# Decode attention with a gated MLP on one core: the first V's load without gate, V31 in halves, wo in seven pieces, loads issued by GpSimd

## The chip, the core and the metric

The kernel runs on one core of a Trainium2 chip. A core has TensorE (PE, matrix products into eight PSUM banks), VectorE (DVE), ScalarE (ACT), GpSimd (POOL) and SyncE (SP), each with an instruction stream of its own; they meet at semaphores. Sixteen DMA engines carry data between device memory (HBM) and the on-chip SBUF of 128 partitions. SyncE, ScalarE and GpSimd can issue loads. The metric is device time of one execution in microseconds.

## The reference

One decode step for two batch rows: attention over a cache of 8192 keys with 32 heads of 128, multiplied by the gate of a small MLP, with a residual. All in float32.

```python
xn = layernorm(x)                                  # x (2, 1, 512)
q = (xn @ wq) as (2, 32 heads, 1, 128)
p = softmax(q . k_cache * 128 ** -0.5)             # k_cache (2, 32, 8192, 128)
s = (p @ v_cache) as (2, 1, 4096) @ wo             # wo (4096, 512)
y = layernorm(xn)
g = silu(gelu_tanh(y @ w1 + b1) @ w2 + b2)         # w1 (512, 1376), w2 (1376, 512)
return x + s * g
```

K and V are 268 MB each; every byte is used once.

## The kernel before, in words

K and V are cut into N = 32 loads each of 8.39 MB: two heads of one batch row a load, 64 partitions for each head, 128 keys in a partition, so a partition receives one contiguous row of 64 KB. In the text K0 to K31 and V0 to V31 are these loads.

Three buffers of that size take turns (lines 120 to 140). KBUF[0] and KBUF[1] take K's even and odd loads; KBUF[1] holds wq first, so K1 is loaded only after the q product (event pq). The third, VB, takes every V but the last, one after the other. Before V0, VB is the home of many small tiles of the start (`boot`): w1, w2, x, xn, y, b2, the copy of q, the selection matrix `sel`, q_all, and `z` and `th` of the gate. V31 goes into KBUF[0], free after K30, and wo into VB after V30.

`op` (line 41) issues one instruction with its waits; `take` (line 38) waits for a count and subtracts it, for use inside the TensorE loop. Line 51 in the profile is the line in `op` that increments the semaphore, so nearly all instructions carry it; they are told apart by tile names.

The order of the work:

- **Start.** SyncE issues w1, w2, the biases, wq and K0 in this order (lines 182 to 189). Layernorms, the w1 product, gelu and the q product follow as these land. Then 64 rows of q are spread to all partitions (`queries`, tiles Q, through banks PB in turn), and w2's product, event `pgate`, ends TensorE's setup. ScalarE copies it to `z` and takes tanh of half of it to `th` (lines 262, 263).
- **Each load n (lines 270 to 306).** VectorE multiplies K by q in place and adds up each key's 128 products (two operations over 16384 elements a partition), then takes the maximum over keys (MX), which TensorE transposes and spreads back (`softmax`), and ScalarE makes the exponentials PZ. TensorE multiplies them with V (`weighted`: 32 products into bank `po`, event p_v; the profile has two rows for each float32 product), ScalarE copies `po` to o4, and TensorE picks each head's own products out of it (event p_t).
- **Loads.** K of n + 2 is issued when the reduction of n is done (k_done); V of n + 1 when the products with V of n are done (p_v). Both are on SyncE, in that order, so a waiting one holds up those behind it.
- **gate and V0 (lines 283 to 290).** In the turn of n = 0, after MX and its negated copy, VectorE computes `gate` = (th + 1) * z. SyncE waits for gate, the last copies of q and pgate, and then issues V0, since z and th lie in VB.
- **End.** V31 is one load; wo comes in four pieces, at columns WO_CUTS of the 32 blocks of rows that lie in a partition, issued after V30's products. After the last product with V, heads are gathered and scaled to `on`, which is multiplied by wo into `acc` (128 small products, 256 rows of the profile; each piece is waited for by itself); VectorE multiplies by gate and adds x, and the result is stored.

PSUM bank 0 is both one of the two PB banks and later `po`, so it is zeroed by VectorE (t["po0"], line 258) after the last q copies from it and ahead of K0's multiplication in VectorE's stream. Bank 4 is `acc` and, early, the place of q's selection (pqa), zeroed after that (t["acc0"], line 259).

Of the kernel before, what the change touches and what calls it, by code (L numbers as in the profile page):

```python
# [13 lines left out]
class Program:  # L14
# [24 lines left out]
    def wait(self, eng, *tokens):  # L39
        for name, v in self.need(eng, tokens):  # L40
            self.engines[eng].wait_ge(self.sem(name), v)

    def take(self, eng, name, v=1):

        self.engines[eng].wait_ge(self.sem(name), v).then_inc(self.sem(name), -v)  # L45

    def op(self, eng, method, *args, waits=(), sig=None, quiet=False, **kwargs):
        need = self.need(eng, waits)
        for name, v in need[:-1]:
            self.engines[eng].wait_ge(self.sem(name), v)  # L50
        ins = getattr(self.engines[eng], method)(*args, **kwargs)  # L51
        for name, v in need[-1:]:
            ins._wait_ge(self.sem(name), v)
        if quiet:
            return None
        name = sig or "own_" + eng
        by = 16 if method == "dma_start" else 1
        ins.then_inc(self.sem(name), by)
        self.counts[name] += by
        return name, self.counts[name]  # L60


def decode_kernel(nc, x, kc, vc, wq, wo, w1, b1, w2, b2, out):
    P = 128
# [4 lines left out]
    U = 2  # L69
    HP = P // U  # L70
    KP = S // HP
    HH = H // U
    N = B * HH
# [5 lines left out]
    JW = 512 // DH  # L79
# [4 lines left out]
    OC = DH // PH  # L84
    BH = B * H
    NPB = 512 // DH
    WO_CUTS = (0, 24, 29, 31, 32)

    pr = Program(nc)
    op, wait, take = pr.op, pr.wait, pr.take  # L90

    def sb(shape, name):
        return nc.alloc_sbuf_tensor(name, list(shape), F32).ap()
# [4 lines left out]
    kf = kc.rearrange("b h s d -> (b h s d)").rearrange("(n p j d) -> n p j d", p=P, j=KP, d=DH)  # L98
    vf = vc.rearrange("b h s d -> (b h s d)").rearrange("(n p j d) -> n p j d", p=P, j=KP, d=DH)
# [3 lines left out]
    KBUF, VB = rows[:2], rows[2]  # L103
    used = [0]

    def boot(p, n):
        a = used[0]
        used[0] += n
        assert used[0] <= KP * DH
        return big[2][:p, a:a + n]  # L110
# [6 lines left out]
    b2_sb = boot(1, D)  # L117
    q_nat = boot(P, NG // QT * 512).rearrange("p (n c) -> p n c", c=512)
    sel = boot(P, P)
    z = boot(P, P)  # L120
    th = boot(P, P)
    q_all = boot(BH, DH)
    wq_sb = big[1].rearrange("p (c n) -> p c n", n=H * DH)
    wo_sb = big[2].rearrange("p (c n) -> p c n", n=D)

    Q = sb([P, N, DH], "Q")
# [4 lines left out]
    mod = sb([P, R], "mod")  # L131
# [3 lines left out]
    x4 = sb([P, P], "x4")  # L135
    gate = sb([P, P], "gate")
    res = sb([P, P], "res")
    xnT = sb([P, ND, B], "xnT")
    yT = sb([P, ND, B], "yT")
    hT = sb([P, NF + 1, B], "hT")  # L140
# [13 lines left out]
    on = sb([P, B, OC], "on")  # L154

    bank = [ps([P, 512], f"bank{i}") for i in range(8)]
    po = bank[0]
# [3 lines left out]
    acc = bank[4][:, :P]  # L161
    OA = bank[5][:, :B * (OC + 1)].rearrange("p (b c) -> p b c", c=OC + 1)
    pgate = bank[6][:, :P]
    ph = bank[7][:, :(NF + 1) * B]
    PQ = [bank[1], bank[2]]
    pxn, py = bank[3][:, :ND * B], bank[5][:, :ND * B]
    pqa = bank[4][:, :P]
    PB = [bank[0], bank[7]]

    PE_EVENTS = ["xnT", "yT", "ph", "pq", "pqa"] + [f"pb{g}" for g in range(N // NPB)] + ["pgate"]  # L170

    def pe(name):
        return "pe_setup", PE_EVENTS.index(name) + 1

    def pe_n(name, n):
        return name, n + 1

    t = {}
# [7 lines left out]
    op("SP", "dma_start", b1_sb[:, NF:], b1[F - P:, None], sig="d_b")  # L186
    t["b"] = op("SP", "dma_start", b2_sb, b2[None, :], sig="d_b")
    op("SP", "dma_start", wq_sb, wq.rearrange("(p c) n -> p c n", p=P), sig="d_wq")
    k_land = {0: op("SP", "dma_start", KBUF[0], kf[0], sig="d_k0")}
    t["x4m"] = op("DVE", "memset", x4, 0.0)  # L190
    for b in range(B):
        t["x4"] = op("ACT", "dma_start", x4[b::R, :], x[b, 0].rearrange("(j n) -> j n", n=P), sig="d_x4",
                     waits=[t["x4m"]])


    a = op("POOL", "memset", ident, 0.0)
# [7 lines left out]
    a = op("DVE", "memset", half, 0.0)  # L204
    for s in range(U):
        t["half"] = op("DVE", "memset", half[HP * s:HP * (s + 1), PH * s:PH * (s + 1)], 1.0, waits=[a])
    a = op("DVE", "memset", sel, 0.0)
    for k in (1, 2, 6):
        t["mem"] = op("DVE", "memset", bank[k], 0.0)
    by_row = ident.rearrange("p (j r) -> p r j", r=R)  # L210
    t["mod"] = op("DVE", "tensor_reduce", out=mod, in_=by_row, axis=AX.X, op=ALU.add, waits=[t["ident"]])
# [1 line left out]
                  op=ALU.add)  # L213
    t["sel"] = op("DVE", "tensor_copy",
                  sel[:, HP:].rearrange("p (b j r) -> p b j r", b=B, r=HG)[:, :, :QT, 0], by_row[:, :B, :],
                  waits=[a])
# [4 lines left out]
    def layernorm(dst, src, name, after):  # L221
# [16 lines left out]
    a = op("DVE", "tensor_tensor", out=gh, in0=ph.rearrange("p (f b) -> p f b", b=B),  # L238
           in1=b1_sb.unsqueeze(2).to_broadcast([P, NF + 1, B]), op=ALU.add, waits=[pe("ph"), t["b"]])
    c = op("DVE", "tensor_mul", gu, gh, gh, waits=[a])  # L240
    c = op("DVE", "tensor_scalar", gu, gu, GELU_A, 1.0, op0=ALU.mult, op1=ALU.add, waits=[c])
    c = op("DVE", "tensor_mul", gu, gu, gh, waits=[c])
# [10 lines left out]
    for g in range(N // NPB):  # L253
        t[f"Q{g}"] = op("ACT", "copy", Q[:, g * NPB:(g + 1) * NPB, :],
                        PB[g % 2].rearrange("p (n d) -> p n d", d=DH), waits=[pe(f"pb{g}")])
        for n in range(g * NPB, (g + 1) * NPB):
            Qt[n] = t[f"Q{g}"]
    t["po0"] = op("DVE", "memset", po, 0.0, waits=[t[f"Q{N // NPB - 2}"]])
    t["acc0"] = op("DVE", "memset", acc, 0.0, waits=[t["qall"]])


    t["z"] = op("ACT", "copy", z, pgate, waits=[pe("pgate")])
    t["th"] = op("ACT", "activation", th, z, AF.Tanh, scale=0.5, waits=[t["z"]])


    op_k1 = op("SP", "dma_start", KBUF[1], kf[1], sig="d_k1", waits=[pe("pq"), ("d_wq", 16)])
    k_land[1] = op_k1

    pending = {}
    for n in range(N):  # L270
        k = KBUF[n % U]
        if n:

            op("ACT", "copy", o4, po, sig="s_o4", waits=[pe_n("p_v", n - 1)])
            t["OT"] = op("ACT", "copy", OT[:, U * (n - 1):U * n], pt[:, :U], waits=[pe_n("p_t", n - 1)])
        qb = Q[:, n, :].unsqueeze(1).to_broadcast([P, KP, DH])
        a = op("DVE", "tensor_tensor", out=k, in0=k, in1=qb, op=ALU.mult, waits=[k_land[n], Qt[n]])
        a = op("DVE", "tensor_reduce", out=SC[n % 2], in_=k, axis=AX.X, op=ALU.add, waits=[a], sig="v_k")
        k_done = a
        op("DVE", "tensor_reduce", out=MX, in_=SC[n % 2], axis=AX.X, op=ALU.max, waits=[a], sig="v_mx")  # L280
        op("DVE", "tensor_reduce", out=nm, in_=pm[:1, :P].rearrange("o (s r) -> o s r", s=U), axis=AX.X,
           op=ALU.max, negate=True, waits=[pe_n("p_m", n)], sig="v_nm")
        if n == 0:
            a = op("DVE", "scalar_tensor_tensor", gate, th, 1.0, z, op0=ALU.add, op1=ALU.mult,
                   waits=[t["th"], t["pool"]])
            t["gate"] = a

            wait("SP", t["gate"], t["sel"], t["qnat"], pe("pgate"))
            op("SP", "dma_start", VB, vf[0], sig="d_v")
            t["v_last"] = None  # L290
        a = op("ACT", "copy", bias, pn[:, :1], waits=[pe_n("p_n", n)])
        sc = SC[n % 2].rearrange("p (t j) -> p t j", j=JW)
        for s in range(U):
            r = slice(HP * s, HP * (s + 1))
            op("ACT", "activation", PZ[r, :, s, :], sc[r], AF.Exp, bias=bias[r], scale=SCALE,
               accum_out=RS[r, n:n + 1], waits=[a, t["pool"]], sig="s_pz")
        m = n + 2
        if m < N:
            k_land[m] = op("SP", "dma_start", KBUF[m % U], kf[m], sig=f"d_k{m % U}", waits=[k_done])
            op("SP", "dma_start", VB, vf[m - 1], sig="d_v", waits=[pe_n("p_v", m - 2)])  # L300
        elif m == N:
            op("SP", "dma_start", KBUF[m % U], vf[N - 1], sig="d_v31", waits=[k_done])
            wait("SP", pe_n("p_v", N - 2))
            wo_v = wo.rearrange("(p c) n -> p c n", p=P)
            for i, (c0, c1) in enumerate(zip(WO_CUTS, WO_CUTS[1:])):
                op("SP", "dma_start", wo_sb[:, c0:c1], wo_v[:, c0:c1], sig=f"d_wo{i}")
    op("ACT", "copy", o4, po, sig="s_o4", waits=[pe_n("p_v", N - 1)])
    t["OT"] = op("ACT", "copy", OT[:, U * (N - 1):], pt[:, :U], waits=[pe_n("p_t", N - 1)])

# [7 lines left out]
    t["on"] = op("DVE", "tensor_tensor", out=on, in0=OA[:, :, :OC], in1=rl.unsqueeze(2).to_broadcast([P, B, OC]),  # L317
                 op=ALU.mult, waits=[a])
    a = op("DVE", "scalar_tensor_tensor", res, acc, 0.5, gate, op0=ALU.mult, op1=ALU.mult,
           waits=[pe_n("p_acc", 0), t["gate"], t["acc0"]])  # L320
    t["res"] = op("DVE", "tensor_add", res, res, x4, waits=[a, t["x4"]])
    for b, eng in enumerate(("SP", "ACT")):
        t[f"o{b}"] = op(eng, "dma_start", out[b, 0].rearrange("(j n) -> j n", n=P), res[b::R, :], sig=f"d_o{b}",
# [70 lines left out]

    def weighted(v, last=False):
        take("PE", "s_pz", U)
        if last:
            nc.tensor.wait_ge(pr.sem("d_v31"), 16)
        else:
            take("PE", "d_v", 16)  # L400
        for i in range(NT):
            j = i % QT
            mm(po[R * j:R * j + U * JW, :], PZ[:, i].rearrange("p s j -> p (s j)"),
               v[:, i * JW:(i + 1) * JW, :].rearrange("p j d -> p (j d)"), start=i < QT, stop=i + QT >= NT,
               sig="p_v" if i == NT - 1 else None)
        take("PE", "s_o4")
        for i in range(JW):
            mm(pt[:, :U], o4[:, i * DH:(i + 1) * DH], mod[:, i:U * JW:JW], start=i == 0, stop=i == JW - 1,
               sig="p_t" if i == JW - 1 else None)

    wait("PE", t["po0"], t["pool"], t["mod"])
    softmax()
    with nc.tensor.Fori(0, N - 1):
        weighted(VB)
# [8 lines left out]
    for i, (c0, c1) in enumerate(zip(WO_CUTS, WO_CUTS[1:])):  # L423
        for c in range(c0, c1):
            for j in range(QT):
                last = c == OC - 1 and j == QT - 1
                mm(acc[R * j:R * j + B, :], on[:, :, c], wo_sb[:, c, j * P:(j + 1) * P], start=c == 0,
                   stop=c == OC - 1, waits=[t["on"], t["acc0"], (f"d_wo{i}", 16)], sig="p_acc" if last else None)


_INS = ["A_x", "A_k_cache", "A_v_cache", "A_wq", "A_wo", "B_w1", "B_b1", "B_w2", "B_b2"]
# [23 lines left out]
```

## Time and profile before

| | us |
|---|---|
| median of three runs | 1325.63 |
| lowest and highest | 1323.99 and 1325.75 |
| the profiled execution | 1324.34 |
| its span, first to last instruction | 1322.9 |
| VectorE busy in it | 1129.2 |
| TensorE busy in it | 396.9 |
| ScalarE busy in it | 70.5 |
| GpSimd busy in it | 1.1 |

Loads move 559.37 MB, 423 GB/s over the span. Times in the profile count from the first instruction. A row of the timeline gives start, duration, engine, line, operation, the tile written and those read, how many such instructions were merged, and in brackets how long the engine had been idle and what ended it. SPq marks SyncE's issuing of a load. A row of DMA issues ends with the time from issue to landing. A row of stretches gives length, busy time (and count) of PE, PEld, DVE, ACT and POOL, the granted TensorE clock, the busy share of the DMA engines and GB/s; a packet's bytes are counted where it begins.

### The profile page before, as it was taken

The page shows a single profiled execution, that of the slowest core. Times are in us where ns is not written, and L with a number is a line of the kernel's source. Part 1 is how long each engine was busy: PE and PEld are TensorE (multiplying, and loading weights), DVE is VectorE, ACT ScalarE, POOL GpSimd, SP SyncE. Part 2 cuts the span into 40 slices and gives each one's busy share as a digit, 9 for nine tenths or more (in the row PEclk, how much of TensorE's full clock was granted, in tenths as well). Part 3 has the DMA queues.
Part 4 walks back from the last instruction along what each step waited for, and adds up shares of the span by engine and source line. Part 5 has one row for each costly group of instructions (what it writes and reads, how often), then busy time and mean ns, then how long its engine had stood idle before and what let it go on. Part 6 is the DMA issues. An engine that isn't in the chain of part 4 may idle for free. (4 is left out here: it accounts for less than half of the span.)

```text
span 1322.9 us, 7003 instructions
## 1 busy us (share of the span) xinstructions
PE 396.9 (30%) x3128; PEld 144.7 (11%) x3128; DVE 1129.2 (85%) x166; ACT 70.5 (5%) x244; POOL 1.1 (0%) x8
## 2 busy tenths in 40 slices
PE   6603211333231233322123332212333221233336
PEld 6300000000000001000000000000000000000003
DVE  1298988888988888898888889888889988888991
ACT  1100000000000000000000000000000000000000
POOL 0000000000000000000000000000000000000000
PEclk9956656666655666665566666556666655666657
DMA  9939999999999999999999999999999999999997
GB/s 413 427 159 444 432 424 442 430 429 442 430 428 442 430 428 442 434 424 442 438 420 442 438 420 442 440 418 440 442 418 440 442 418 440 442 418 440 442 418 318
DMA packets 10704, 559.51 MB, mean 423 GB/s; under 512 B 1459, under 2 KB 1475, under 8 KB 1862
## 3 DMA queue, kind: packets, MB, share of 16 engines
q1 hardware_dynamic: 10666, 559.36, 97.9%
q8 instruction: 6, 0.10, 0.0%
q14 instruction: 4, 0.03, 0.0%
q10 hardware_dynamic: 28, 0.01, 0.0%
HBM read 559.37 MB, written 0.00 MB: 423 GB/s over the span
## 5 line engine op out<-in xcount | busy, mean ns | idle before, releaser
L51 DVE TENSOR_TENSOR big<-big,Q 128x16384 f32<-128x16384 f32 x32 | 551.2, 17224 | 96.1 <-DMA big<-in_A_k_cache_dram 96.1
L51 DVE TENSOR_REDUCE sc<-big 128x128 f32<-128x16384 f32 x32 | 551.0, 17220 | 1.1
L51 PE MATMUL bank<-big,PZ 128*8 128x512 f32 x2048 | 287.9, 725 | 689.2 <-PEq L45 686.7
L51 PEld LDWEIGHTS bank<-big,PZ 128*8 128x8 f32 x2048 | 59.7, 102 | 890.4 <-issue 887.8
L51 ACT COPY o<-bank 128x512 f32<-128x512 f32 x32 | 18.7, 585 | 939.8 <-PE bank L51 939.8
L51 PE MATMUL bank<-ident,MX 128*1 128x128 f32 x32 | 11.9, 372 | 172.1 <-PEq L45 172.1
L51 PE MATMUL bank<-mod,o 128*128 128x2 f32 x256 | 32.8, 250 | 25.7 <-PEq L45 25.7
L51 PEld LDWEIGHTS bank<-mod,o 128*128 128x128 f32 x256 | 31.0, 191 | 54.4 <-issue 54.4
L51 ACT ACTIVATE PZ<-sc,bias 64x128 f32<-64x128 f32 x64 | 25.5, 399 | 1.9
L51 DVE TENSOR_REDUCE nm<-bank 1x2 f32<-1x128 f32 x32 | 8.9, 279 | 17.8 <-PE bank L51 17.8
L51 DVE MEMSET bank<- 128x512 f32 (+1 forms) x5 | 2.1, 421 | 25.3 <-ACT Q L51 25.1
L51 PEld LDWEIGHTS bank<-ident,MX 128*1 128x1 f32 x32 | 2.5, 79 | 174.1 <-issue 174.1
L51 PE MATMUL bank<-yT,big 128*128 128x2 f32 x88 | 19.9, 364 | 1.9 <-DMA big<-in_B_w_dram 1.9
L51 PEld LDWEIGHTS bank<-yT,big 128*128 128x128 f32 x88 | 19.9, 322 | 2.0 <-DMA big<-in_B_w_dram 2.0
L51 DVE TENSOR_TENSOR gh<-bank,b_sb 128x22 f32<-128x22 f32 x1 | 0.2, 181 | 22.7 <-PE bank L51 22.7
L51 PE MATMUL bank<-nm,srow 1*64 1x1 f32 x128 | 12.0, 243 | 14.8 <-PEq L45 14.8
L51 ACT COPY bias<-bank 128x1 f32<-128x1 f32 x32 | 5.1, 160 | 205.3 <-PE bank L51 205.3
L51 PEld LDWEIGHTS bank<-nm,srow 1*64 1x64 f32 x128 | 10.2, 200 | 24.2 <-issue 24.2
L51 DVE TENSOR_TENSOR Z<-blk,OT 128x256 f32<-128x256 f32 x1 | 0.4, 425 | 14.0 <-ACT OT L51 14.0
L51 ACT ACTIVATION_READ_ACCUMULATOR PZ<-sc,bias 64x1 f32 x64 | 11.8, 185 | 0.0
L51 PE MATMUL bank<-big,xnT 128*2 128x512 f32 x64 | 9.1, 732 | 6.9 <-DMA big<-in_A_wq_dram 6.9
L51 DVE TENSOR_REDUCE MX<-sc 128x1 f32<-128x128 f32 x32 | 9.1, 286 | 1.1
(64 smaller groups left out, 69.4 us busy)
## 6 DMA issues: line engine op xcount, KB each, us to landing
big<-in_A_wo_dram SPq DMA_DIRECT2D x1, 6144.0 KB, 23.7
big<-in_B_w_dram SPq DMA_DIRECT2D x1, 2752.0 KB, 9.4
big<-in_B_w_dram SPq DMA_DIRECT2D x1, 2560.0 KB, 14.9
big<-in_A_wo_dram SPq DMA_DIRECT2D x1, 1280.0 KB, 26.4
big<-in_A_k_cache_dram SPq DMA_DIRECT2D x32, 42.9
big<-in_A_v_cache_dram SPq DMA_DIRECT2D x32, 29.5
big<-in_A_wo_dram SPq DMA_DIRECT2D x1, 512.0 KB, 27.2
big<-in_B_w_dram SPq DMA_DIRECT2D x1, 256.0 KB, 15.3
```

Source lines behind the costliest of these rows:

```text
L51: ins = getattr(self.engines[eng], method)(*args, **kwargs)
```

## The change

- `z` and `th` get tiles of their own. V0 waits for the copies of q and for pgate, no longer for gate.
- Every load from V0 on (K from K2 on, all V, wo) is issued by GpSimd, in the same order and with the same waits, with `single_packet=True`: the rows that one DMA engine carries for a load form one packet. The loads of before V0, K0 and K1 among them, stay on SyncE.
- V's landing is passed on: SyncE waits for it and raises a second semaphore (`relay`), which TensorE takes.
- V31 comes in two halves of each partition's row; TensorE waits for the second ahead of the 17th of its 32 products.
- wo comes in seven pieces instead of four.
- PB's first bank is bank 3 instead of 0, pqa lies in bank 5; banks 0 and 4 are zeroed at the very start, with the other three, and the two later zeroings go.

```diff
+    def relay(self, eng, token, name):
+
+        self.engines[eng].wait_ge(self.sem(token[0]), token[1]).then_inc(self.sem(name), 1)
+        self.counts[name] += 1
...
-    WO_CUTS = (0, 24, 29, 31, 32)
+    WO_CUTS = (0, 10, 18, 24, 28, 30, 31, 32)
+    V_CUTS = (0, KP // 2, KP)
...
-    z = boot(P, P)
-    th = boot(P, P)
...
+    z = sb([P, P], "z")
+    th = sb([P, P], "th")
...
-    pqa = bank[4][:, :P]
-    PB = [bank[0], bank[7]]
+    pqa = bank[5][:, :P]
+    PB = [bank[3], bank[7]]
...
-    for k in (1, 2, 6):
+    for k in (1, 2, 6, 4, 0):
         t["mem"] = op("DVE", "memset", bank[k], 0.0)
...
-    t["po0"] = op("DVE", "memset", po, 0.0, waits=[t[f"Q{N // NPB - 2}"]])
-    t["acc0"] = op("DVE", "memset", acc, 0.0, waits=[t["qall"]])
...
-            wait("SP", t["gate"], t["sel"], t["qnat"], pe("pgate"))
-            op("SP", "dma_start", VB, vf[0], sig="d_v")
-            t["v_last"] = None
+            wait("POOL", t["sel"], t["qnat"], pe("pgate"))
+            pr.relay("SP", op("POOL", "dma_start", VB, vf[0], sig="d_v", single_packet=True), "s_v")
...
         if m < N:
-            k_land[m] = op("SP", "dma_start", KBUF[m % U], kf[m], sig=f"d_k{m % U}", waits=[k_done])
-            op("SP", "dma_start", VB, vf[m - 1], sig="d_v", waits=[pe_n("p_v", m - 2)])
+            k_land[m] = op("POOL", "dma_start", KBUF[m % U], kf[m], sig=f"d_k{m % U}", waits=[k_done],
+                           single_packet=True)
+            a = op("POOL", "dma_start", VB, vf[m - 1], sig="d_v", waits=[pe_n("p_v", m - 2)], single_packet=True)
+            pr.relay("SP", a, "s_v")
         elif m == N:
-            op("SP", "dma_start", KBUF[m % U], vf[N - 1], sig="d_v31", waits=[k_done])
-            wait("SP", pe_n("p_v", N - 2))
+            for i, (c0, c1) in enumerate(zip(V_CUTS, V_CUTS[1:])):
+                op("POOL", "dma_start", KBUF[m % U][:, c0:c1], vf[N - 1][:, c0:c1], sig=f"d_v31{i}", waits=[k_done],
+                   single_packet=True)
+            wait("POOL", pe_n("p_v", N - 2))
             wo_v = wo.rearrange("(p c) n -> p c n", p=P)
             for i, (c0, c1) in enumerate(zip(WO_CUTS, WO_CUTS[1:])):
-                op("SP", "dma_start", wo_sb[:, c0:c1], wo_v[:, c0:c1], sig=f"d_wo{i}")
+                op("POOL", "dma_start", wo_sb[:, c0:c1], wo_v[:, c0:c1], sig=f"d_wo{i}", single_packet=True)
...
-        if last:
-            nc.tensor.wait_ge(pr.sem("d_v31"), 16)
-        else:
-            take("PE", "d_v", 16)
+        if not last:
+            take("PE", "s_v")
         for i in range(NT):
+            if last and i * JW in V_CUTS:
+                nc.tensor.wait_ge(pr.sem(f"d_v31{V_CUTS.index(i * JW)}"), 16)
             j = i % QT
...
-    wait("PE", t["po0"], t["pool"], t["mod"])
+    wait("PE", t["mem"], t["pool"], t["mod"])
```

More of the change, by code (lines that the diff above doesn't have):

```diff
@@ L188, in decode_kernel @@
     op("SP", "dma_start", wq_sb, wq.rearrange("(p c) n -> p c n", p=P), sig="d_wq")
-    k_land = {0: op("SP", "dma_start", KBUF[0], kf[0], sig="d_k0")}
+    k_land = {0: op("SP", "dma_start", KBUF[0], kf[0], sig="d_f0")}
     t["x4m"] = op("DVE", "memset", x4, 0.0)
@@ L257, in decode_kernel @@
             Qt[n] = t[f"Q{g}"]
-    t["po0"] = op("DVE", "memset", po, 0.0, waits=[t[f"Q{N // NPB - 2}"]])
-    t["acc0"] = op("DVE", "memset", acc, 0.0, waits=[t["qall"]])
     t["z"] = op("ACT", "copy", z, pgate, waits=[pe("pgate")])
     t["th"] = op("ACT", "activation", th, z, AF.Tanh, scale=0.5, waits=[t["z"]])
-    op_k1 = op("SP", "dma_start", KBUF[1], kf[1], sig="d_k1", waits=[pe("pq"), ("d_wq", 16)])
+    op_k1 = op("SP", "dma_start", KBUF[1], kf[1], sig="d_f1", waits=[pe("pq"), ("d_wq", 16)])
     k_land[1] = op_k1
@@ L319, in decode_kernel @@
     a = op("DVE", "scalar_tensor_tensor", res, acc, 0.5, gate, op0=ALU.mult, op1=ALU.mult,
-           waits=[pe_n("p_acc", 0), t["gate"], t["acc0"]])
+           waits=[pe_n("p_acc", 0), t["gate"]])
     t["res"] = op("DVE", "tensor_add", res, res, x4, waits=[a, t["x4"]])
@@ L427, in decode_kernel @@
                 mm(acc[R * j:R * j + B, :], on[:, :, c], wo_sb[:, c, j * P:(j + 1) * P], start=c == 0,
-                   stop=c == OC - 1, waits=[t["on"], t["acc0"], (f"d_wo{i}", 16)], sig="p_acc" if last else None)
+                   stop=c == OC - 1, waits=[t["on"], t["mem"], (f"d_wo{i}", 16)], sig="p_acc" if last else None)
 _INS = ["A_x", "A_k_cache", "A_v_cache", "A_wq", "A_wo", "B_w1", "B_b1", "B_w2", "B_b2"]
```

## The prediction

> **What bounds the kernel now.** I read the page's slices and DMA queue first.
>
> ```profile
> span 1322.9 us, 7003 instructions
> DMA  9939999999999999999999999999999999999997
> GB/s 413 427 159 444 432 424 442 430 429 442 430 428 442 430 428 442 434 424 442 438 420 442 438 420 442 440 418 440 442 418 440 442 418 440 442 418 440 442 418 318
> q1 hardware_dynamic: 10666, 559.36, 97.9%
> ```
>
> The reader sees a kernel bound by its loads. The sixteen DMA engines are full in every slice but two: the third (66 to 99 us), where they move 159 GB/s, and the last. So I asked for the stretches around the third slice and one plain iteration, and for the instructions and landings there.
>
> ```profile
> 73.00:74.00 1.00, 0.00 (x0) 0.00 (x0) 1.00 (x1) 0.00 (x0) 0.00 (x0) 0.50 0.31 131
> 78.00:90.00 12.00, 0.00 (x0) 0.00 (x0) 12.00 (x1) 0.00 (x0) 0.00 (x0) 0.50 0.00 0
> 93.00:94.00 1.00, 0.38 (x4) 0.32 (x4) 1.00 (x3) 0.21 (x2) 0.00 (x0) 0.50 0.00 0
> 94.00:95.00 1.00, 0.00 (x0) 0.00 (x0) 1.00 (x1) 0.93 (x4) 0.00 (x0) 0.50 2.85 983
> 600.00:638.70 38.70, 11.35 (x77) 3.34 (x77) 35.01 (x4) 1.89 (x7) 0.00 (x0) 0.59 1.00 434
> ```
>
> The last three columns are granted clock, DMA share and GB/s. No packet starts from 74 to 94 us. In an iteration of 38.70 us the share is 1.00 and the rate 434 GB/s, while VectorE works 35.01 us of it. The next rows are, in order, K0's and K1's issue, the landings of K0, K1 and V0 (us after issue), VectorE's first multiplication, the gate's last matmuls, gate on VectorE, the second multiplication, V0's issue, V0's first use, and SyncE's wait.
>
> ```profile
> 4.27 0.44 SPq L51 DMA_DIRECT2D big<-in_A_k_cache_dram  x1
> 46.38 0.33 SPq L51 DMA_DIRECT2D big<-in_A_k_cache_dram  x1
> big<-in_A_k_cache_dram SPq DMA_DIRECT2D x1, 52.2
> big<-in_A_k_cache_dram SPq DMA_DIRECT2D x1, 29.6
> big<-in_A_v_cache_dram SPq DMA_DIRECT2D x1, 21.9
> 57.52 17.21 DVE L51 TENSOR_TENSOR big<-big,Q 128x16384 f32<-128x16384 f32 x1
> 61.00 0.40 PE L51 MATMUL bank<-big,ones 1*2 1x128 f32 x8
> 74.76 17.22 DVE L51 TENSOR_REDUCE sc<-big 128x128 f32<-128x16384 f32 x1
> 93.06 0.27 DVE L51 SCALAR_TENSOR_TENSOR gate<-big 128x128 f32<-128x128 f32 x1
> 93.26 17.20 DVE L51 TENSOR_TENSOR big<-big,Q 128x16384 f32<-128x16384 f32 x1
> 93.36 0.33 SPq L51 DMA_DIRECT2D big<-in_A_v_cache_dram  x1
> 115.38 9.25 PE L51 MATMUL bank<-big,PZ 128*8 128x512 f32 x64 [21.72 <-PEq L45]
> SPq L51 <- DVE gate L51: 31.9, 1, 31.9
> ```
>
> K0 lands at 4.27 + 52.2 = 56.47, K1 at 46.38 + 29.6 = 75.98. V0 is issued only at 93.36, when VectorE has come past two 17.2 us operations to the 0.27 us gate; it lands at 93.36 + 21.9 = 115.26. That is the hole.
>
> Then a plain iteration (V's issue and landing, K's, the work between) and the end.
>
> ```profile
> 629.53 0.33 SPq L51 DMA_DIRECT2D big<-in_A_v_cache_dram  x1
> big<-in_A_v_cache_dram SPq DMA_DIRECT2D x1, 28.9
> 634.93 0.33 SPq L51 DMA_DIRECT2D big<-in_A_k_cache_dram  x1
> big<-in_A_k_cache_dram SPq DMA_DIRECT2D x1, 42.9
> 639.13 17.23 DVE L51 TENSOR_TENSOR big<-big,Q 128x16384 f32<-128x16384 f32 x1 [3.07 <-DMA big<-in_A_k_cache_dram]
> 656.39 17.22 DVE L51 TENSOR_REDUCE sc<-big 128x128 f32<-128x16384 f32 x1
> 667.66 0.33 SPq L51 DMA_DIRECT2D big<-in_A_v_cache_dram  x1
> ```
>
> V lands at 658.4, K at 677.8: 19.4 us apart, in the order of issue. Each was queued 20 us and more ahead, so the queue never runs dry; VectorE waits 3.07 us per iteration for K. From V0 (115.26) to V31 (1297.09, below) 61 more loads land: 1181.83 / 61 = 19.37 us each.
>
> ```profile
> L51 SPq DMA_DIRECT2D big<-in_A_wo_dram x4: 328/434/436, 1287.9 to 1289.2; - x4
> 1295.59 0.18 ACT L51 ACTIVATION_READ_ACCUMULATOR PZ<-sc,bias 64x1 f32 x1
> 1297.09 8.90 PE L51 MATMUL bank<-big,PZ 128*8 128x512 f32 x64 [2.56 <-DMA big<-in_A_v_cache_dram]
> 1310.16 0.22 DVE L51 TENSOR_TENSOR on<-bank,rl 128x64 f32<-128x64 f32 x1
> 1311.66 8.54 PE L51 MATMUL bank<-big,on 128*2 128x128 f32 x256 [1.74 <-DMA big<-in_A_wo_dram]
> 1320.27 0.29 DVE L51 SCALAR_TENSOR_TENSOR res<-bank,gate 128x128 f32<-128x128 f32 x1 [9.89 <-PE bank L51]
> big<-in_A_wo_dram SPq DMA_DIRECT2D x1, 6144.0 KB, 23.7
> big<-in_A_wo_dram SPq DMA_DIRECT2D x1, 256.0 KB, 27.3
> ```
>
> At the end V31 holds TensorE back 1.3 us behind the last exponential (1295.77), and wo's 24-column piece (1287.89 + 23.7 = 1311.6) by 1.3 us behind `on` (1310.38).
>
> **The change, part by part.**
>
> *V0 without gate.* V0 now waits for pgate (61.40) and the copies before it. Its issue at about 61.5 is 14.5 us ahead of K1's landing, so V0 lands one load after K1: 75.98 + 19.37 = 95.35 instead of 115.26. Gain **19.9 us**, for everything behind it, if nothing else runs dry. I check what is late next. K0's multiplication no longer follows the zeroing of `po`, which waited for the last Q copies; it starts with K0 at 56.5 instead of 57.52, and its reduction ends at 56.5 + 34.46 = 90.96. K2 is issued then, 4.4 us before V0 lands; SyncE's V0 had its first bytes 0.6 to 1.6 us after issue. So GpSimd may take up to some 3 us longer for nothing. V1 follows TensorE's 9.25 us on V0: 104.6, while K2 fills the queue to 114.7. The second reduction starts after a multiplication at 92.2 and ends at 126.7, so K3 is 7.4 us ahead of V1's landing (134.1). After that VectorE's 35.74 us per iteration (34.46 and 1.28 between) is shorter than two loads, 38.74, so its lead grows by 3 us each time until it waits for K as now.
>
> *Zeroing of two more banks early.*
>
> ```profile
> L51 DVE MEMSET bank<- 128x512 f32 (+1 forms) x5 | 2.1, 421 | 25.3 <-ACT Q L51 25.1
> ```
>
> Five memsets in place of three add 2 x 0.42 = 0.84 us to VectorE's start and leave the place ahead of K0's multiplication. Everything set back there ends in K1's issue at 46.38, ten us before K0 lands. Nothing. The moved z and th, PB and pqa change addresses alone.
>
> *GpSimd issues the loads.* 62 K and V loads and wo leave SyncE's queue for GpSimd's, which was idle after 2 us. Order and waits are the same, so what queues behind a waiting load is the same next load. A V is queued 658.4 - 648 = 10 us before the engines reach it (they finish the K ahead at 639.1, V's issue is 629.53), a K 23 us before. An issue several times SyncE's 0.33 us is covered. Per load in the stream, GpSimd's cost isn't in this trace; the nearest rows are the loads themselves, which took from 19.37 (mean) to 19.51 (K1 after K0). I take **0**, with +-0.1 us for 62 loads, +-6 us. The low side is open because one packet an engine might shed something between the eight rows that an engine moves for one load.
>
> The Trainium skill, DMA: Bandwidth & Descriptors, section Where 436 GB/s comes from, sets a ceiling of 435 GB/s; this trace's 434 leaves 0.3 per cent, an estimated 3 us by that page, for any gain in the stream.
>
> *The relay.* SyncE passes V's landing on by one semaphore step. It delays TensorE's start, which has 10 us of cover for the next V; V31 isn't relayed. Nothing.
>
> *V31 in halves.* Its first half lands some 9.7 us sooner, so TensorE starts on the last exponential at 1295.8: 1.27 us gained. The second half has landed at 1297.05, before half of the matmuls are done. `on` comes at 1309.1.
>
> *wo in seven.* The first ten columns land 10/32 of a load after V31, about 1303, before `on`. TensorE starts at 1309.15 in place of 1311.66; its 8.57 us end at 1317.7. The last column lands at 1289.2 + 27.3 = 1316.5, so it isn't late if the matmuls keep that pace. If they ran faster, the landing would set 1316.7. Gain with the halves 2.5 to 3.5; I take **2.6 us**. GpSimd's nine issues at the end have at least nine us before V31's landing, and 19 us for the last.
>
> Sum: 19.9 + 2.6 = 22.5 us off the profiled execution's 1324.34, so 1301.8. The median shown is 1.29 above that execution, which I add: **1303**.
>
> **The rivals.**
>
> *A. Forecast: the stream keeps its pace.* 1297 to 1309 with the +-6 us. For it: share 1.00 across the borders of loads today, and 3 to 20 us of cover for each issue. Chance 0.68.
>
> *B. K2 starved at the start.* Had GpSimd not written K2's requests in the 1.28 us between the reduction and VectorE's next two-input multiplication, and were it kept out until that ends (92.24 + 17.2 = 109.4), K2 would land at 109.4 + 21.9 = 131.3 instead of 114.7. The loss is 16.6 us, the time 1303 + 16.6 = 1320. Later iterations are safe: K's issue at 634.93 is 4.2 us ahead of the multiplication at 639.13, and V's issues (629.53, 667.66) fall into reductions. Against it: these rows show no work on GpSimd beside VectorE at all, and only this one load is exposed. Chance 0.10. The Trainium skill, SBUF — State Buffer, section Who interferes with whom, is where such a rule stands: a VectorE instruction with two SBUF inputs contends with a GpSimd instruction that reads SBUF, and its section on the two separate sides warns that GpSimd-issued loads starve behind some VectorE operations. It infers that a tensor_tensor spares descriptor writing; no run here shows it yet.
>
> *C. A border between loads costs time (the slower side).* If an engine had to finish one load's packet before it takes up the next, each of 62 loads would pay the start that V0 paid after the hole, 0.6 to 1.6 us. At 0.9 us: 62 x 0.9 = 56 us, less 22.5, gives 1359. It decides from 22.5 / 62 = 0.36 us a load; below that it only eats the gain. For it: packets of a whole load are new. Against it: one queue feeds the engines now without a gap. Chance 0.17 (0.14 slower, 0.03 about even).
>
> *D. V0 doesn't come early.* GpSimd's first load could need more than the 12.5 us between 61.5 and the last bytes of K1 (74). Each further us costs one, up to the 19.9: about 1313. Chance 0.05.
>
> **How the numbers follow.** The likeliest is A, 1303. B and D lie within 1295 to 1321; with nearly all of A that makes 0.8, and C is left out. A measurement of this kernel tells about 0.2 per cent (2.7 us) from no change. Faster: A, B, D, 0.83; within: 0.03; slower: 0.14, from C.
>
> **What would show it.** Right: bytes in every slice from the second on; V0 landing near 95 and K2 near 115; period 38.7; VectorE waiting 3 us for K in mid run; TensorE's last V at the last exponential; wo's matmuls directly behind `on`. Wrong: a hole near 95 to 110 (B), a period above 39.1 or share under 1.00 (C; a period under 38.6 would beat the forecast), or a hole from 74 on (D).

## The result, and the profile after

| | us |
|---|---|
| before, median of 4 | 1324.81 |
| after, median of 4 | 1302.96 (1301.68 to 1305.26) |
| ratio, 95% interval | 0.9837, 0.9819 to 0.9855 |
| after, the profiled execution | 1303.78 |
| its span | 1302.2 |

The page of the changed kernel, slices and queues:

```profile
span 1302.2 us, 7038 instructions
DMA  9999999999999999999999999999999999999997
GB/s 402 446 417 427 439 431 435 435 435 433 429 437 433 437 429 435 433 435 433 435 435 433 433 431 437 429 439 431 433 433 435 435 433 435 427 437 433 437 424 326
q0 software_dynamic: 9952, 528.49, 93.9%
q1 hardware_dynamic: 1162, 30.88, 5.6%
```

The third slice, 159 GB/s before, now moves 417. GpSimd's queue (q0) carries 528 of 559 MB, SyncE's (q1) what lies before V0. Timeline and landings of the start:

```profile
56.73 17.23 DVE L56 TENSOR_TENSOR big<-big,Q 128x16384 f32<-128x16384 f32 x1 [25.00 <-DMA big<-in_A_k_cache_dram]
62.12 0.68 POOL L56 DMA_DIRECT2D big<-in_A_v_cache_dram  x1 [60.42 <-ACT th L56]
big<-in_A_v_cache_dram POOLq DMA_DIRECT2D x1, 33.3
91.52 0.54 POOL L56 DMA_DIRECT2D big<-in_A_k_cache_dram  x1 [28.72 <-DVE sc L56]
big<-in_A_k_cache_dram POOLq DMA_DIRECT2D x1, 24.1
92.49 17.20 DVE L56 TENSOR_TENSOR big<-big,Q 128x16384 f32<-128x16384 f32 x1
105.03 0.53 POOL L56 DMA_DIRECT2D big<-in_A_v_cache_dram  x1 [12.98 <-PE bank L56]
```

V0 is issued at 62.12, thirty us ahead of gate (92.29), and lands at 62.12 + 33.3 = 95.42. (The trace puts the wait's end down to th; th isn't in V0's wait list, pgate is, which ended 0.7 us earlier.) K2 lands at 91.52 + 24.1 = 115.6. In mid run, the same kernel:

```profile
400.00:787.00 387.00, 109.08 (x770) 32.53 (x770) 350.10 (x41) 18.90 (x70) 10.63 (x20) 0.62 1.00 434
614.82 0.53 POOL L56 DMA_DIRECT2D big<-in_A_k_cache_dram  x1 [4.70 <-DVE sc L56]
618.74 17.23 DVE L56 TENSOR_TENSOR big<-big,Q 128x16384 f32<-128x16384 f32 x1 [3.06 <-DMA big<-in_A_k_cache_dram]
657.45 17.23 DVE L56 TENSOR_TENSOR big<-big,Q 128x16384 f32<-128x16384 f32 x1 [3.08 <-DMA big<-in_A_k_cache_dram]
```

Two multiplications start 38.71 us apart, the share is 1.00 at 434 GB/s, and VectorE waits 3.06 us for K: all as before. An issue takes GpSimd 0.53 us where SyncE took 0.33. The end of the changed kernel, with granted clock, DMA share and GB/s in the last columns of the stretches:

```profile
1238.00 17.23 DVE L56 TENSOR_TENSOR big<-big,Q 128x16384 f32<-128x16384 f32 x1 [3.08 <-DMA big<-in_A_k_cache_dram]
1272.51 0.29 DVE L56 TENSOR_REDUCE MX<-sc 128x1 f32<-128x128 f32 x1
1275.54 9.62 PE L56 MATMUL bank<-big,PZ 128*8 128x512 f32 x64 [1.38 <-PEq L45]
1277.05 0.54 POOL L56 DMA_DIRECT2D big<-in_A_wo_dram  x1 [7.49 <-issue]
big<-in_A_wo_dram POOLq DMA_DIRECT2D x1, 256.0 KB, 19.4
1290.50 9.05 PE L56 MATMUL bank<-big,on 128*2 128x128 f32 x256 [0.61 <-DVE on L56]
1299.62 0.29 DVE L56 SCALAR_TENSOR_TENSOR res<-bank,gate 128x128 f32<-128x128 f32 x1 [9.27 <-PE bank L56]
...
1276.00:1280.00 4.00, 4.00 (x24) 0.50 0.99 425
1288.00:1290.00 2.00, 1.86 (x8) 0.50 1.02 430
1290.50:1294.00 3.50, 3.50 (x68) 0.50 0.98 401
1295.00:1299.00 4.00, 4.00 (x156) 1.00 0.10 35
```

K31's multiplication began at 1258.38 before and begins at 1238.00 now: 20.4 us earlier. From there to the span's end it was 64.5 us and is 64.2. So nearly the whole gain lies ahead of K31, and the tail gave 0.3 in this pair of executions. Nothing in it waits for a load any more (V31's products start 0.15 us after the last exponential, wo's 0.14 after `on`, and the last column landed at 1277.05 + 19.4 = 1296.45), but TensorE's clock is at half in two stretches of it.

### The profile page after: what moved, and what is told of

It reads as the page before. It is cut to its first block, busy times and chain, and to the rows that moved or that the text cites. A ratio compares the mean times of both kernels' runs of the same rounds, so it can differ in the third digit from the quotient of the medians.

```text
span 1302.2 us, 7038 instructions
## 1 busy us (share of the span) xinstructions
PE 402.4 (31%) x3128; PEld 146.6 (11%) x3128; DVE 1129.3 (87%) x166; ACT 70.7 (5%) x244; POOL 38.4 (3%) x78
## 3 DMA queue, kind: packets, MB, share of 16 engines
q0 software_dynamic: 9952, 528.49, 93.9%
## 5 line engine op out<-in xcount | busy, mean ns | idle before, releaser
L56 PE MATMUL bank<-big,PZ 128*8 128x512 f32 x2048 | 291.9, 734 | 619.3 <-PEq L45 619.3
L56 POOL DMA_DIRECT2D big<-in_A_v_cache_dram x33 | 17.7, 536 | 968.5 <-PE bank L56 902.7
L56 POOL DMA_DIRECT2D big<-in_A_k_cache_dram x30 | 15.9, 531 | 231.3 <-DVE sc L56 231.3
L56 PE MATMUL bank<-yT,big 128*128 128x2 f32 x88 | 19.9, 364 | 0.7 <-DMA big<-in_B_w_dram 0.7
L56 PEld LDWEIGHTS bank<-yT,big 128*128 128x128 f32 x88 | 19.9, 322 | 0.8 <-DMA big<-in_B_w_dram 0.8
L56 DVE TENSOR_TENSOR gh<-bank,b_sb 128x22 f32<-128x22 f32 x1 | 0.2, 181 | 21.4 <-PE bank L56 21.4
```

## The experiments

The theory: the hole ahead of V0 was worth its 20 us and nothing else counts, since the stream of loads keeps its pace whoever issues it; the tail's 2 us were lost to TensorE's clock. The rivals: GpSimd's one-packet loads carry part of the gain; GpSimd is kept out by VectorE (B); the tail waits for data.

**V0 without gate, alone.** The kernel before with

```diff
-    z = boot(P, P)
-    th = boot(P, P)
...
+    z = sb([P, P], "z")
+    th = sb([P, P], "th")
...
-            wait("SP", t["gate"], t["sel"], t["qnat"], pe("pgate"))
+            wait("SP", t["sel"], t["qnat"], pe("pgate"))
```

> One part alone: the kernel before with z and th in tiles of their own and V0 not waiting for gate; SyncE issues every load, V31 is whole, wo in four pieces. Theory (the gain is the hole ahead of V0): V0 issued near 61.5, landing near 95.5, period 38.70, 1304 to 1306 us, 19.9 under before. Rival (GpSimd's one-packet loads carry part of the gain): less than 15 us under before, that is over 1310.

Measured: 1304.90 (1303.91 to 1305.70), before 1324.97 beside it: 20.1 us, ratio 0.9842 (0.9827 to 0.9857). The start of this kernel:

```profile
61.52 0.33 SPq L51 DMA_DIRECT2D big<-in_A_v_cache_dram  x1
big<-in_A_v_cache_dram SPq DMA_DIRECT2D x1, 34.1
91.71 0.33 SPq L51 DMA_DIRECT2D big<-in_A_k_cache_dram  x1
big<-in_A_k_cache_dram SPq DMA_DIRECT2D x1, 24.6
```

V0 lands at 95.6 and K2 at 116.3, as in the changed kernel or later. Two edits, to z and th and to one wait, carry the gain.

**Gate put back, alone.** The changed kernel with

```diff
-            wait("POOL", t["sel"], t["qnat"], pe("pgate"))
+            wait("POOL", t["gate"], t["sel"], t["qnat"], pe("pgate"))
```

> One part undone: the changed kernel with V0 waiting for gate again; GpSimd issues the loads, halves and seven pieces stay. Theory: the hole from 74 to 94 us is back, V0 lands near 115, the time is that of the changed kernel plus 19 to 20: 1321 to 1324. Rival (issue by GpSimd in itself gains): under 1315.

Measured: 1324.40, one run, 21.4 above the changed kernel and at the time before (1324.97 beside it). The stretch row of this kernel:

```profile
74.00:92.00 18.00, 0.30 (x1) 0.08 (x1) 17.51 (x2) 0.00 (x0) 0.00 (x0) 0.50 0.00 0
```

No byte moves in 18 us. With the hole back, GpSimd's issue, halves and pieces together show no gain beyond a run's scatter.

**Rows as packets of their own.** The changed kernel with `single_packet=True` left out of every load.

> One part undone: the changed kernel with GpSimd's loads, but without the one packet an engine. Theory (a load's border and its rows cost nothing that can be measured): period 38.70, 1301 to 1305. Rival (one packet an engine sheds something between rows, or saves GpSimd work): a period over 38.8 and a time 3 us or more above the changed kernel's; or, if one packet costs, a period under 38.65.

Measured: 1303.70 (1302.20 to 1305.24), 387 us of mid run again at 434 GB/s and share 1.00; multiplications from 348.88 to 1239.25 make 890.37 / 23 = 38.71 us each. The queue of this kernel:

```profile
q0 software_dynamic: 9952, 528.49, 93.8%
```

The flag is worth nothing that shows. What one packet an engine is worth is not shown: the page counts 9952 packets with the flag and 9952 without it, so no trace here tells whether the flag joined the rows of an engine into one packet.

**SyncE issues everything.** The changed kernel with

```diff
-            pr.relay("SP", op("POOL", "dma_start", VB, vf[0], sig="d_v", single_packet=True), "s_v")
+            op("SP", "dma_start", VB, vf[0], sig="d_v")
...
-            take("PE", "s_v")
+            take("PE", "d_v", 16)
```

and the other loads likewise.

> One part undone: the changed kernel with every load issued by SyncE, without relay, the rest as changed. Theory (who issues is worth nothing): 1301 to 1305, period 38.70, V0 landing near 95.5. Rival (GpSimd's issue costs or gains): 0.2 per cent or more away from the changed kernel, either way.

Measured: 1302.16 (1301.91 to 1303.62), ratio 0.9828 (0.9815 to 0.9842), 0.8 us under the changed kernel and inside its interval of about +-2.4. Here too, who issues the loads makes no difference that these runs resolve; the lowest median of the changed kernel's relatives is one without GpSimd, but not by more than the scatter.

**V0 into an empty queue beside the multiplication (rival B).** The changed kernel without SyncE's K1, and

```diff
             pr.relay("SP", op("POOL", "dma_start", VB, vf[0], sig="d_v", single_packet=True), "s_v")
+            k_land[1] = op("POOL", "dma_start", KBUF[1], kf[1], sig="d_k1", waits=[("d_wq", 16)], single_packet=True)
```

> The changed kernel with K1 issued by GpSimd right after V0, so that V0 goes into an empty queue at 62 us, inside VectorE's first multiplication with two SBUF inputs (57 to 74). Theory (GpSimd writes its requests beside that operation): V0 moves bytes by 64 and lands near 84, the time is some 8 us above the changed kernel's, about 1311. Rival B (GpSimd is kept out until the multiplication ends): no bytes before 74, V0 lands near 96, about 1322.

Measured: 1309.20, one run, 6.2 above the changed kernel's median (about 8 was expected). In this kernel's timeline, landings and stretches:

```profile
56.90 17.23 DVE L56 TENSOR_TENSOR big<-big,Q 128x16384 f32<-128x16384 f32 x1 [24.79 <-DMA big<-in_A_k_cache_dram]
60.20 0.67 POOL L56 DMA_DIRECT2D big<-in_A_v_cache_dram  x1 [58.50 <-ACT th L56]
big<-in_A_v_cache_dram POOLq DMA_DIRECT2D x1, 22.6
60.00:61.00 1.00, 0.00 (x0) 0.00 (x0) 1.00 (x1) 0.16 (x1) 0.80 (x2) 1.00 0.00 0
61.00:62.00 1.00, 0.00 (x0) 0.00 (x0) 1.00 (x1) 0.00 (x0) 0.40 (x1) 1.00 3.07 918
```

GpSimd issues at 60.20, in the middle of the multiplication (56.90 to 74.13), and the engines take up the load within 2 us; it lands at 82.8. B is out: from an empty queue, issue to landing took 22.6 us beside an operation with two inputs in SBUF, where SyncE's V0 before took 21.9. The Trainium skill, SBUF — State Buffer, section Who interferes with whom, infers that a tensor_tensor doesn't hold up the writing of requests; this row bears the inference out.

**V0 at 74.** The changed kernel with V0 also waiting for K0's multiplication.

```diff
+        if n == 0:
+            t["m0"] = a
...
-            wait("POOL", t["sel"], t["qnat"], pe("pgate"))
+            wait("POOL", t["m0"], t["sel"], t["qnat"], pe("pgate"))
```

> The changed kernel with V0 also waiting for K0's multiplication, so that GpSimd issues it near 74 instead of 62. Theory (an issue costs nothing as long as K1 still fills the engines, and then one us per us): V0 starts within 1 to 2 us of the last engine's end with K1 (74 to 75.5), lands at 95.4 to 97, and the time is 0 to 2 us above the changed kernel's. Rival (the gain comes from an early issue itself, not from a full queue): a loss in proportion, 12 of the 31 us between 62 and 93, that is 7 us or more.

Measured: 1305.28, one run, 2.3 above the changed kernel's median. V0 is issued at 74.39 and lands 22.4 later, at 96.79: 1.4 us after the changed kernel's, for an issue 12.3 us later. Its stretch from 74 to 75 shows 0 GB/s, so its queue did run dry, for about a microsecond. A loss of 7 us or more, in proportion to the delay, didn't come: what counts is that the queue doesn't run dry. (The time's 2.3 us alone are within the scatter of the changed kernel's runs.)

**The old tail.** The changed kernel with

```diff
-    WO_CUTS = (0, 10, 18, 24, 28, 30, 31, 32)
-    V_CUTS = (0, KP // 2, KP)
+    WO_CUTS = (0, 24, 29, 31, 32)
+    V_CUTS = (0, KP)
```

> One part undone: the changed kernel with V31 whole and wo in four pieces as before. First theory (halves and pieces are worth their 2.6 us, but TensorE's clock took most of it in the one profiled execution): products with V31 start 1.2 us later after K31's multiplication than in the changed kernel, wo's products wait for a landing, and the time is 1 to 3 us longer, the exact sum going by the clock granted in the last 30 us. Rival (the tail is worth nothing whatever the clock): within 0.5 us of the changed kernel.

Measured: 1304.79 (1304.40 to 1307.32), 1.8 above the changed kernel's median, which two intervals of some 2 us don't resolve. Its rows can be compared with the changed kernel's step by step:

```profile
1274.18 0.29 DVE L56 TENSOR_REDUCE MX<-sc 128x1 f32<-128x128 f32 x1
1278.40 8.74 PE L56 MATMUL bank<-big,PZ 128*8 128x512 f32 x64 [2.57 <-DMA big<-in_A_v_cache_dram]
1292.95 8.39 PE L56 MATMUL bank<-big,on 128*2 128x128 f32 x256 [1.89 <-DMA big<-in_A_wo_dram]
```

V31's products start 4.22 us after the last maximum (3.03 with halves), wo's wait for a landing (not with seven pieces): the two waits are there. But V31's products take 8.74 against 9.62 and wo's 8.39 against 9.05. The span of this run is 1.8 longer than the changed kernel's mostly because its last maximum came 1.7 us later, before the tail.

**TensorE kept busy, too long.** The changed kernel with

```diff
+    WARM = (48, 14)
...
+    def warm(k):
+        for i in range(k):
+            mm(bank[7][:B, :P], ident[:, :B], ident)
+
-    with nc.tensor.Fori(0, N - 1):
+    with nc.tensor.Fori(0, N - 2):
         weighted(VB)
         softmax()
+    weighted(VB)
+    warm(WARM[0])
+    softmax()
+    warm(WARM[1])
     weighted(KBUF[0], last=True)
```

> The changed kernel with 48 idle 128-column products of the identity on TensorE ahead of the last maximum's transposition and 14 ahead of the products with V31, into a bank that nothing reads. Theory (TensorE's half clock in the last 30 us ate the 2.3 us that the tail didn't give): the granted clock is 1.00 from V31's products on, they take 6.9 us in place of 9.62, the gathering products 1.1 in place of 1.9, wo's products end with the last landing, and the time is 2.5 to 3.5 us under the changed kernel, about 1300. Rival (the tail waits for data, not for TensorE's clock): the same time as the changed kernel within 0.5 us.

Measured: 1310.35, 7.4 us slower than the changed kernel: the expectation missed. The rows show why:

```profile
1269.66 10.64 PE L56 MATMUL bank<-ident 128*2 128x128 f32 x96
1273.64 0.29 DVE L56 TENSOR_REDUCE MX<-sc 128x1 f32<-128x128 f32 x1
1280.24 0.27 PE L56 MATMUL bank<-ident,MX 128*1 128x128 f32 x1
```

I had priced an idle product by wo's products, of which the stretches show 48 rows, that is 24 products, in a us at full clock. The idle ones took 10.64 / 48 = 0.22 us each at full clock, and the transposition of the last maximum (ready at 1273.93) stood behind them until 1280.24. The kernel says nothing on the tail's gain, but V31's products took 7.2 us (1284.02 to 1291.26), less than in any kernel so far. So:

**The gaps filled, and no more.** The same with warm(16) and warm(5) for 48 and 14, and warm(3), warm(4), warm(2) after V31's products, after p_t and after the gathering.

> The changed kernel with idle products of the identity on TensorE (0.22 us each at full clock, as the 48 of the run before took 10.64 us), now cut to the gaps: 16 ahead of the last maximum's transposition, 5 ahead of V31's products, 3, 4 and 2 in the three short gaps between V31's products and wo's, all into a bank that nothing reads. Theory (the half clock ate the tail's gain): granted clock 1.00 through V31's products, the gathering and wo's first products; V31's products near 7 us, wo's end set by the last landing and not by TensorE; from the last maximum to the end of the span 27.5 to 28 us in place of 29.7, the time 1.5 to 2 us under the changed kernel's. Rival (the tail waits for data): 29.7 us again.

> The same idle products in the kernel with all loads issued by SyncE. Theory: from the last maximum to the end 27 to 28 us in place of 28.5, and a time of 1300 to 1302, the lowest of all kernels here; GpSimd against SyncE makes no difference beyond 1 us. Rival (GpSimd's loads are worth something): 2 us or more above the run with the same products and GpSimd's loads.

Measured: 1302.36 (1301.90 to 1302.88) and, with SyncE issuing, 1302.69 (1302.38 to 1302.78). The tail of the first, and V31's products in the second:

```profile
1273.83 0.29 DVE L56 TENSOR_REDUCE MX<-sc 128x1 f32<-128x128 f32 x1
1276.66 7.05 PE L56 MATMUL bank<-big,PZ 128*8 128x512 f32 x64 [0.20 <-PEq L45]
1297.93 0.40 PE L56 MATMUL bank<-big,on 128*2 128x128 f32 x8 [0.22 <-DMA big<-in_A_wo_dram]
...
1276.70:1283.70 7.00, 7.00 (x66) 1.00 1.00 423
1284.00:1287.00 3.00, 2.76 (x24) 1.00 0.95 404
1288.00:1291.00 3.00, 3.00 (x58) 0.50 0.98 414
...
1276.34 8.53 PE L56 MATMUL bank<-big,PZ 128*8 128x512 f32 x64
```

In the first, V31's products take 7.05 us at clock 1.00, and wo's last ones wait for the last landing: here the tail is bound by data. In the second the idle products didn't hold the clock: it was 0.50 from 1276 to 1279, and V31's products took 8.53. From the last maximum to the span's end, one profiled execution each, with how long TensorE took over V31's products and over those that gather the heads ahead of `on`:

| kernel | last maximum | span | between | V31's products | gathering |
|---|---|---|---|---|---|
| before (old tail) | 1292.89 | 1322.9 | 30.0 | 8.90 | 1.05 |
| gate only (old tail) | 1273.41 | 1304.4 | 31.0 | 9.58 | 1.87 |
| old tail | 1274.18 | 1304.0 | 29.8 | 8.74 | 1.05 |
| after | 1272.51 | 1302.2 | 29.7 | 9.62 | 1.86 |
| gate back (new tail) | 1293.02 | 1322.9 | 29.9 | 9.76 | 1.86 |
| rows apart (new tail) | 1273.76 | 1303.6 | 29.8 | 9.68 | 1.87 |
| SyncE issues (new tail) | 1272.18 | 1300.7 | 28.5 | 8.42 | 1.05 |
| V0 before K1 (new tail) | 1279.65 | 1307.7 | 28.1 | 8.75 | 1.05 |
| V0 at 74 (new tail) | 1274.20 | 1304.0 | 29.8 | 9.62 | 1.86 |
| new tail, gaps filled | 1273.83 | 1301.1 | 27.3 | 7.05 | 1.05 |
| the same, SyncE issues | 1273.52 | 1301.3 | 27.8 | 8.53 | 1.05 |

The old tail takes 29.8 to 31.0 us, mean 30.3; the new one without idle products 28.1 to 29.9, mean 29.3; with them 27.3 and 27.8. Within each tail, the long times are those in which the gathering ran at half clock. Like compared with like, the two edits to the tail show: with a gathering of 1.86 or 1.87 us the old tail took 31.0 and the new one 29.7 to 29.9, with one of 1.05 the old took 29.8 and 30.0 and the new 28.1 and 28.5. That is 1.1 to 1.9 us at a like clock.

So the theory holds for the tail by the rows of the first filled kernel: with the clock at 1.00 through V31's products and the gathering, 27.3 us in place of the changed kernel's 29.7, so the clock had taken about two us. The second filled kernel doesn't test it. Its `on` starts 15.5 us after the last maximum, as in SyncE's kernel without idle products (15.6), and the 0.7 us between these two kernels come later. The expected times didn't come: neither filled kernel is told from the changed one (1302.96) or from SyncE's (1302.16). In the profiled executions the last maximum itself came 1.0 to 1.7 us later in these two than in those; the other executions have no trace. The two filled kernels differ by 0.3 us: GpSimd against SyncE again makes no difference that shows. Of the versions tried, none is shown to beat the changed kernel.

## Why the prediction was right, point by point

**The hole, 19.9 us.** Right in place, cause and size. V0 lands at 95.42 (95.35 was worked out), K31's multiplication starts 20.4 us earlier, and the gate edits alone gave 20.1.

**K2's cover.** Right: K2 landed at 115.6 against 114.7, and no later than with SyncE's issue (116.3). It landed 20.2 us behind V0 and not 19.4, but with SyncE's issue it was 20.7: the extra isn't GpSimd's.

**Two more zeroings early, PB and pqa.** Nothing, as worked out: TensorE still waits for w1's landing, 0.70 us now and 1.95 before, and K0's multiplication starts at K0's landing (56.73; 56.5 was said).

**GpSimd and one packet at 0, +-6 us.** The middle was right and the width wasn't needed: 38.70 us an iteration with GpSimd and with SyncE, 38.71 with rows apart. Rival C (a border between loads) is out with it, rival D by V0's landing, and B by the run with the empty queue and by K2's landing. One reading on the way was wrong: "queued 20 us and more ahead" holds for K alone. V is queued ten us ahead of its turn (629.53 to 639.1), as the prediction itself says further on, and ten were enough.

**The tail, 2.6 us.** This term was mis-sized: it measured 0.3 in the profiled execution, 1.0 between the means of the table, and 1.1 to 1.9 at a like clock. The step that failed is "TensorE starts at 1309.15 in place of 1311.66; its 8.57 us end at 1317.7", together with V31's 8.9 us: I moved TensorE's work to an earlier start and kept its durations. The two waits did go: 1.2 us ahead of V31's products, 1.1 ahead of wo's. But V31's products took 9.62 instead of 8.90 (0.7 lost), the gathering 1.86 instead of 1.05 (0.8), wo's 9.05 instead of 8.54 (0.5). The stretches show it: in the changed kernel the clock is 0.50 from 1288 to 1290, when the heads are gathered; in the kernel before it held through the same work and fell after it, between 1311 and 1312, at the start of wo's products. V31's products began at half clock in both; by the mean clock of the slices in which it rose (the last two rows, before and after), full clock came some 3.8 us after their start before, and some 5.2 after.

```profile
1306.00:1311.00 5.00, 2.08 (x16) 1.00 0.87 374
1311.70:1314.20 2.50, 2.50 (x52) 0.50 0.92 374
1300.00:1301.00 1.00, 1.00 (x8) 0.57 1.48 639
1280.00:1281.00 1.00, 1.00 (x8) 0.62 1.02 434
```

The Trainium skill, TensorE: Matmul & The Clock Gate, Part 1, says that the clock is set by the activity in windows of some 3.4 us that run freely, not from the work's start. That agrees with a fall that comes at different steps of the same tail (at the start of wo's products before and with SyncE's issue, ahead of the gathering after), but no run here shows the windows themselves. In the first kernel with filled gaps the clock fell between 1287 and 1288, although TensorE had been 0.92 busy from 1284 to 1287; why is open.

**The sum.** 1301.8 was said for the profiled execution, which took 1303.78: the tail gave 2.3 less, the stream 0.5 more, and 0.14 lies outside the span. That the median came out at 1302.96 against 1303 is partly luck: four runs scatter over 3.6 us, and 1.29 had been added for the runs' offset before.

## What to carry to other kernels

When loads fill the engines, look for the slice that is empty and for what its first load waits for; two tiles of 64 KB that share a load's buffer can hold up a stream of 500 MB, and freeing it is worth the length of the hole, whoever issues the load. An issue is early enough when it comes before the queue runs dry: here one that came 12 us later, with the engines idle for about a us, had its load land 1.4 us later. A term that moves TensorE's products must give their duration at half and at full clock as its two ends, since an earlier start can fall into the slower one.

## What the runs showed of the hardware, unexpected

- GpSimd's seventh piece of wo was issued 7.49 us after the sixth, with no semaphore to wait for ("issue" in its row above), and came through at 1277.05, when V31 had landed. With V31 whole and wo in four, four pieces went out in 2.20 us without a pause. The other runs with halves, seven pieces and GpSimd's issue show the same pause, of 6.4 to 7.5 us; SyncE's seven went out in 3.46 us without one. It looks like a bound on requests that GpSimd may have outstanding; this was not tried further, and cost nothing, as that piece's data was due 19 us later.
- The start of the stream scatters: in the eight kernels that issue V0 near 62 us, the last K multiplication starts between 1237.67 and 1239.67, though their iterations all take 38.70 or 38.71 us, and the 2 us are there already at the eighth multiplication (308.76 to 310.75). No run here shows where they arise.
